# One order and one choice of buffers replaced by another: gated attention and its channel mixer on one TensorE

## The chip, the cores and the metric

The program runs on 1 core of a Trainium2 chip. The metric is device microseconds of one execution. Three runs of the kernel before took 421.2, 421.72 and 422.78 us; the median is 421.72 us. One further execution was taken by the hardware profiler, and every duration below is from it.

## The reference

Four batches, 8 heads, 768 time steps, head width 48, all in float32. Attention is a recurrence over time on a complex state, and its result is the input of a mixer with squared-ReLU and a sigmoid gate:

```
scale = minimum(mag, 0.999) / (mag + 1e-06)          # mag = |a_re + i a_im|
S_re, S_im = ar*S_re - ai*S_im + k (x) v, ar*S_im + ai*S_re
y[t] = q[t] @ S_re                                   # -> x: [batch, time, 8*48]
xk = mu_k*x + (1-mu_k)*x_prev;  xr = mu_r*x + (1-mu_r)*x_prev
v = maximum(xk @ w_k, 0)**2 @ w_v                    # 384 -> 1024 -> 384
out = sigmoid(xr @ w_r) * v
```

## The kernel before, in words

**Units.** The work is cut into eight units u = 0 to 7 of 384 time steps (two for each batch). A unit has three parts. `gate(u)` is work of ScalarE and VectorE: it loads a_re, a_im, k and q (`g`), takes logarithms, scans them over time (L668, L695), and multiplies k and q by the exponentials and by cosine and sine (L685, L730). Its intermediate tiles are called `m`, `ph`, `sq` and `r`. `attend(u)` is TensorE's work on small tiles: transposes of k (`tr`), sums of k times v for the state (`up`), scores (`sc`, masked by VectorE to `pt` at L986) and values (`y`). ScalarE takes the values out of PSUM to `xt` and `ys` (L1046). `mix(u)` makes `xk` and `xr` from `xt` and multiplies them by the weights.

**The mixer on TensorE.** From unit 1 on, each float32 factor is split in two float32r parts (`x` at L361 and L364, `h` at L441 and L445, `w` at L559 and L562), and each product is three matmuls over 128 rows and 384 columns. A product of one 128-row block, `z` (L388), is 9 matmuls. ScalarE applies ReLU (`r`, L429) and squares (`h`, L433), and 9 more matmuls (`o`, L469) add it into three accumulators. Unit 0 does its mixer in plain float32 instead (`z` at L384, `o`): its inputs come from L343 on ScalarE and L347 on VectorE, and the whole weights `wx` are put together from 16-bit pieces by a cast on ScalarE (L535) and a VectorE operation (L540).

**Large and small products.** In what follows `z` and `o` are the large products and `tr`, `up`, `sc` and `y` the small ones. All of a kind are emitted by one line or two, and TensorE alternates between both sorts, because `attend(u)` of a unit runs between the mixer products of the unit before it.

**What sets the order.** Every operation is recorded in a `Plan`, and `ORDER` gives each one a number. `Plan.run` emits them by rising number. The five engine queues then run in that order, and semaphores that the framework adds hold each instruction until its inputs and its buffer are ready.

**Buffers.** A tile is taken from a pool by a tag. Five PSUM banks share the tag `ps`, three `x` buffers, four `r`, two `hx` (which hold the split `h`), two `kt`, two `pt`, four `v` and two `g`. Which of them a new tile gets is the framework's pick; a tile whose buffer still has a reader waits.

A second path, which steps through time in a loop, stands behind a test at the end (L1127); it does not run with these inputs.

Of the kernel before, what the change touches and what calls it, by code (L numbers as in the profile page):

```python
# [22 lines left out]
C = H * D  # L23
# [12 lines left out]
YS = 1  # L36
# [132 lines left out]
}  # L169
PIECE = 2  # L170
GP = 2
HB = 2
R_XK = 1
RB = 4
SIG = 2.5
# [1058 lines left out]
```

## Time and profile before

| | us |
|---|---|
| median of three runs | 421.72 |
| span of the profiled execution (first to last instruction) | 420.5 |
| TensorE (PE) busy | 370.6, 88% |
| VectorE (DVE) busy | 328.6, 78% |
| ScalarE (ACT) busy | 316.6, 75% |
| first matmul starts at | 29.24 |
| last group of matmuls starts at | 409.02 |

The profiled execution has no time of its own beside its span: its 420.5 us stand 1.2 us below the median, and the rest of a run lies around the span.

How to read it. PE, DVE, ACT and SP are TensorE, VectorE, ScalarE and the queue of SyncE that issues the DMAs. PEld is TensorE's loading of weights, which overlaps its matmuls. A busy PE is not a PE at its peak, because matmuls are pipelined and their ends are modelled; from one group's start to the next group's start is the sound measure of how long a group took. [...]

### The profile page before, as it was taken

What the parts mean: (1) busy time and instruction counts of PE and PEld (TensorE: products, weight loads), DVE (VectorE), ACT (ScalarE), POOL (GpSimd) and SP (SyncE); (2) the same over time, 40 slices, a digit from 0 to 9 for tenths busy, and PEclk for the clock granted to TensorE, in tenths of its full rate; (3) what the DMA queues carried; (4) which work ended last, traced back from release to release, by engine and by line L of the source; (5) the groups of instructions that cost most, each with busy time, mean ns of one, the idle gap of its engine ahead of it and who ended that gap; (6) DMA issues with size and microseconds to landing.
All of it is one profiled execution on the core that took longest, in us unless ns stands there. A gap on an engine that the chain in (4) does not pass through costs nothing.

```text
span 420.5 us, 13399 instructions
## 1 busy us (share of the span) xinstructions
PE 370.6 (88%) x5705; PEld 333.5 (79%) x5705; DVE 328.6 (78%) x528; ACT 316.6 (75%) x620; POOL 8.2 (2%) x32
## 2 busy tenths in 40 slices
PE   0018849998999999999999999999999999999992
PEld 0017725776689999999999999899999999999991
DVE  3988899698899989888999789889979694564231
ACT  6999998976998899679987996789776833345221
POOL 6000000000000000000000000000000000000000
PEclk9999969998999999999999999999999999999998
DMA  7998462451444082334343353513140440100101
GB/s 257 412 373 209 133 223 77 89 187 45 142 104 148 8 256 57 86 153 143 82 127 139 133 139 105 228 29 89 49 107 4 105 95 19 53 0 2 57 2 65
DMA packets 22996, 49.72 MB, mean 118 GB/s; under 512 B 4848, under 2 KB 16368, under 8 KB 22928
## 3 DMA queue, kind: packets, MB, share of 16 engines
q1 hardware_dynamic: 22928, 48.78, 37.3%
q8 instruction: 47, 0.77, 0.8%
q14 instruction: 21, 0.17, 0.1%
HBM read 31.06 MB, written 4.72 MB: 85 GB/s over the span
## 4 chain that ended last, share of the span: by engine, by line
PE 63%; ACT 19%; DVE 5%; issue 4%; DVEq 0%; ACTq 0%
PE z L388 25%; PE o L469 17%; PE y L1011 8%; PE up L853 4%; PE sc L970 3%; ACT L248 2%; ACT sq L255 2%; PE tr L821 2%; ACT ph L255 1%; ACT r L255 1%; PE sc L965 1%; ACT r L429 1%; ACT h L433 1%; PE z L384 1%; ACT x L361 1%
## 5 line engine op out<-in xcount | busy, mean ns | idle before, releaser
L388 PE MATMUL z<-x,w 128*128 128x384 f32 x693 | 130.6, 340 | 0.5 <-ACT kt L834 0.4
L388 PEld LDWEIGHTS z<-x,w 128*128 128x128 f32 x693 | 119.4, 188 | 2.7 <-ACT kt L834 0.7
L469 PE MATMUL o<-hx,w 128*128 128x384 f32 x504 | 99.4, 342 | 0.0
L469 PEld LDWEIGHTS o<-hx,w 128*128 128x128 f32 x504 | 86.2, 188 | 1.1
L429 ACT ACTIVATE r<-z 128x384 f32<-128x384 f32 x64 | 30.5, 488 | 32.6 <-PE z L388 28.3
L970 PE MATMUL sc<-g 48*64 48x64 f32 x1200 | 26.1, 228 | 30.9 <-DVE g L730 29.8
L970 PEld LDWEIGHTS sc<-g 48*64 48x64 f32 x1200 | 23.3, 137 | 34.6 <-DVE g L730 30.0
L730 DVE TENSOR_TENSOR g<-g,r 128x768 f32<-128x768 f32 (+1 forms) x24 | 41.5, 1755 | 6.7 <-ACT r L255 6.4
L441 DVE CAST hx<-h 128x384 fp32r<-128x384 f32 x44 | 16.1, 366 | 28.9 <-ACT h L433 17.1
L433 ACT ACTIVATE h<-r 128x384 f32<-128x384 f32 x64 | 33.1, 526 | 2.8 <-DMA out_t<-y 1.6
L255 ACT ACTIVATE sq<-m 128x1152 f32<-128x1152 f32 (+1 forms) x30 | 28.3, 970 | 6.7 <-DVE m L651 4.6
L445 DVE TENSOR_TENSOR hx<-h,hx 128x384 fp32r<-128x384 f32 x56 | 30.4, 553 | 2.2 <-PE z L388 1.5
L248 ACT ACT_TABLE_LOAD x24 | 30.8, 1283 | 1.2 <-PEq L1223 0.8
L361 ACT CAST x<-xm 128x384 fp32r<-128x384 f32 x42 | 21.3, 515 | 11.6 <-DVE xm L353 6.3
L384 PE MATMUL z<-x,wx 128*128 128x384 f32 x66 | 24.4, 524 | 5.4 <-DVE x L347 5.4
L364 DVE TENSOR_TENSOR x<-xm,x 128x384 fp32r<-128x384 f32 x42 | 23.0, 553 | 7.8 <-ACT x L361 7.6
L1011 PE MATMUL y<-q,state 112*48 112x64 f32 (+1 forms) x704 | 25.4, 226 | 3.1 <-ACT xt L1046 1.9
L1011 PEld LDWEIGHTS y<-q,state 112*48 112x48 f32 (+1 forms) x704 | 22.8, 133 | 6.4 <-issue 4.0
L353 DVE SCALAR_TENSOR_TENSOR xm<-dx,mu_sb,xt 128x384 f32<-128x384 f32 x42 | 25.4, 614 | 0.6
L853 PEld LDWEIGHTS up<-v,kt 64*48 64x48 f32 (+1 forms) x1216 | 21.5, 127 | 5.1 <-issue 3.0
L384 PEld LDWEIGHTS z<-x,wx 128*128 128x128 f32 x66 | 13.4, 208 | 14.5 <-issue 7.3
L853 PE MATMUL up<-v,kt 64*64 64x48 f32 (+1 forms) x1216 | 24.0, 217 | 0.0
(89 smaller groups left out, 557.6 us busy)
## 6 DMA issues: line engine op xcount, KB each, us to landing
g<-in_gat SPq DMA_DIRECT2D x18, 768.0 KB, 5.7
raw<-in_w_all SPq DMA_DIRECT2D x9, 767.8 KB, 10.1
g<-in_gat SPq DMA_DIRECT2D x12, 384.0 KB, 8.1
v<-in_vt SPq DMA_DIRECT2D x24, 192.0 KB, 3.5
out_t<-y SPq DMA_DIRECT2D x24, 192.0 KB, 2.5
q<-g SPq DMA_DIRECT2D x84, 48.0 KB, 2.2
q<-g SPq DMA_DIRECT2D x28, 144.0 KB, 3.1
q<-g SPq DMA_DIRECT2D x40, 72.0 KB, 2.3
```

Of the source, the lines that this page charges most:

```text
L248: nc.scalar.add_instruction(mybir.InstLoadActFuncSet(name=nc.get_next_instruction_name(), act_func_set_id=n, engine=mybir.EngineType.Activ ...
L255: nc.scalar.activation(out=out, in_=in_, func=func, **kw)
L384: nc.tensor.matmul(z, lhsT=wx[s[0]][:, s[1]], rhs=hi[which][:, ct], start=ct == 0, stop=ct == NT - 1)
L388: nc.tensor.matmul(z, lhsT=wt[s[0]][:, part, s[1]], rhs=r[which][:, ct], start=n == 0, stop=n == 3 * NT - 1)
L429: nc.scalar.activation(out=t["r", j], in_=t["f", j], func=AF.Relu, scale=1.0 / W_SCALE)
L433: nc.scalar.activation(out=t["h", j], in_=t["r", j], func=AF.Square)
L445: nc.vector.tensor_tensor(out=t["lo", j], in0=t["h", j], in1=t["hi", j].bitcast(F32), op=ALU.subtract)
L469: nc.tensor.matmul(tiles["o", mt], lhsT=w, rhs=r, start=j == 0 and n == 0, stop=j == NJ - 1 and n == len(parts) - 1)
L730: nc.vector.tensor_tensor(out=g[:, d, 2 * i:2 * i + 2], in0=g[:, d, 2:4], in1=t["r"][:, 1 - i, d].unsqueeze(2).to_broadcast([P, k, 2, U]), ...
L853: nc.tensor.matmul(t["up", c, s][i * HR:(KR if i else HR), h * D:(h + 1) * D], lhsT=keys, rhs=V[u][c][r, h * D:(h + 1) * D], start=True, s ...
L970: nc.tensor.matmul(y, lhsT=g[:, 2 * i, q], rhs=g[:, 2 * i + 1, q], start=i == 0, stop=i == 1)
L1011: nc.tensor.matmul(t["y", team][s][rows, h // 2 - team[0], c], lhsT=lhsT[:, cols], rhs=rhs, start=(s, h % 2) not in begun, stop=stop)
```

## The change

All numbers of `ORDER` are replaced by others. The operations, their shapes and their engines are the same. A second table, `HOMES`, states for each tile that takes turns on a few buffers which of them it uses, and each buffer becomes a tag of its own, with one tile at a time. The numbers of buffers stay (five PSUM banks, three `x`, four `r`, two of each of the rest). Of the order's table one row stands here for all.

```
--- before.py
+++ after.py
-    ("w", 0): (36, 41,),
+    ("w", 0): (54, 62,),
...
+BANKS = dict(ps=PB, x=XB, r=RB, hx=HB, kt=KB, pt=PTS, v=VB, g=GB)
+HOMES = {
+    "g": "01010101",
+    "kt": "010101101001001010010101",
...
+    def home(self, slot):
+
+        tag, n = slot
+        return f"{tag}{self.homes[tag][n] if tag in self.homes else n % BANKS[tag]}"
...
-    ps = ctx.enter_context(pool("ps", 5, space=PSUM))
+    ps = ctx.enter_context(pool("ps", 1, space=PSUM))
...
+    def bank(slot, name):
+        return ps.tile([P, 512], F32, tag=home(slot), name=name)
...
-                t["f", j] = ps.tile([P, 512], F32, tag="ps", name="z")[:, :U]
+                t["f", j] = bank(sp, "z")[:, :U]
...
-                t["hx", j] = mp["h"].tile([P, 2, U], F32R, tag="hx", name="hx", bufs=HB)
+                t["hx", j] = mp["h"].tile([P, 2, U], F32R, tag=home(sx), name="hx")
...
+            plan[0].homes = HOMES
             plan[0].run(ORDER)
```

Three places show what the new order does. Line numbers after the change are higher by 29 to 36. In the rows a shape is that of the output, as partitions by elements.

On ScalarE (ACT), ahead of unit 0's mixer. `hx<-raw` is a cast for the weights, `sq` a step of unit 1's gate, `xt` and `ys` the values taken from PSUM, `x<-xt` the inputs of unit 0's first product. Before:

```order
L535 CAST hx<-raw 128x768
L535 CAST hx<-raw 128x384
L1046 ACTIVATE xt,stat<-y 48x3x64 x4
L343 ACTIVATE x<-xt,mu_98 128x384
L255 ACTIVATE sq<-m 128x3x384
L343 ACTIVATE x<-xt,mu_98 128x384 x2
L255 ACTIVATE sq<-m 128x3x384
```

After:

```order
L570 CAST hx<-raw 128x768 x2
L378 ACTIVATE x<-xt,mu_98 128x384 x2
L1081 ACTIVATE xt,stat<-y 48x3x64 x4
L378 ACTIVATE x<-xt,mu_98 128x384 x2
L284 ACTIVATE sq<-m 128x3x384 x2
```

The gate step that stood between the inputs stands behind them. In all, two casts for weights (one of 768 columns, one of 384) and one gate step that stood ahead of the third input of the first product stand behind it, and one more `x<-xt` stands ahead of it.

On ScalarE again, at the values of unit 1. Here `ph` is the arctangent of unit 2's gate, behind a load of its function table. Before:

```order
L255 ACTIVATE sq<-m 128x3x384 x2
L248 ACT_TABLE_LOAD
L255 ACTIVATE ph<-ph 128x1152
L1046 ACTIVATE xt,stat<-y 112x2x3x64 x2
L1046 ACTIVATE ys,stat<-y 112x3x64 x2
```

After:

```order
L1081 ACTIVATE xt,stat<-y 112x2x3x64
L284 ACTIVATE sq<-m 128x3x384 x2
L277 ACT_TABLE_LOAD
L284 ACTIVATE ph<-ph 128x1152
L1081 ACTIVATE xt,stat<-y 112x2x3x64
```

One of the two takings of `y` moved ahead of four gate instructions.

On TensorE, at the second half of unit 4's attention. Before, ahead of the scores and in the middle of the values:

```order
L853 MATMUL up<-v,kt 48x48 x2
L469 MATMUL o<-hx,w 128x384 x9
L388 MATMUL z<-x,w 128x384 x18
L970 MATMUL sc<-g 64x64 x24
L965 MATMUL sc<-q_93 64x64 x12
L1011 MATMUL y<-q_92,state_87 64x64
...
L1011 MATMUL y<-pt,v 48x64 x2
L469 MATMUL o<-hx,w 128x384 x9
L1011 MATMUL y<-q_93,state_87 64x64
```

After:

```order
L888 MATMUL up<-v,kt 48x48 x2
L423 MATMUL z<-x,w 128x384 x54
L504 MATMUL o<-hx,w 128x384 x9
L423 MATMUL z<-x,w 128x384 x27
L504 MATMUL o<-hx,w 128x384 x9
L1046 MATMUL y<-q_92,state_87 64x64
...
L1046 MATMUL y<-pt,v 48x64 x2
L1005 MATMUL sc<-g 64x64 x24
L1000 MATMUL sc<-q_93 64x64 x12
L1046 MATMUL y<-q_93,state_87 64x64
```

Scores and values now follow each other without a large product between them, and the large products stand together in longer runs. Over the whole order, TensorE goes from a small product back to a large one 59 times before (24 of them from a transpose) and 30 times after (14 from a transpose). Runs of 18 or more `o` matmuls: 2 before; 14 after, of which 4 have 27.

## Rows read from the trace of the kernel before

**Rows 1.** Waits of PE: waiter, line, releaser, total us, times, longest.

```profile
PE z L384 <- DVE x L347: 5.4, 1, 5.4
PE y L1011 <- ACT xt L1046: 1.9, 1, 1.9
```

**Rows 2.** Busy us in stretches: PE, PEld, DVE, ACT, POOL, granted clock, DMA share, GB/s.

```profile
42.00:63.00 21.00, 13.76 (x346) 10.46 (x339) 18.71 (x38) 20.16 (x45) 0.38 (x1) 0.84 0.53 176
...
105.00:126.00 21.00, 20.57 (x239) 15.23 (x238) 18.09 (x27) 20.94 (x37) 0.00 (x0) 1.00 0.45 123
...
127.00:409.00 282.00, 281.40 (x4247) 266.91 (x4245) 221.69 (x356) 201.08 (x400) 1.36 (x13) 1.00 0.30 90
```

**Rows 3.** PE in order of time: start, us, group; ahead of unit 0's mixer and in it.

```profile
52.70 0.56 PE L1011 MATMUL y<-pt,v 64*64 64x64 f32 x24
58.66 9.89 PE L384 MATMUL z<-x,wx 128*128 128x384 f32 x24 [5.39 <-DVE x L347]
68.39 2.10 PE L469 MATMUL o<-h,wx 128*128 128x384 f32 x6
```

**Rows 4.** ACT in order of time, ahead of unit 0's mixer.

```profile
52.48 1.55 ACT L535 CAST hx<-raw 128x768 f16<-128x768 bf16 x2
...
56.01 0.62 ACT L343 ACTIVATE x<-xt,mu 128x384 f32<-128x384 f32 x1
56.53 1.15 ACT L255 ACTIVATE sq<-m 128x1152 f32<-128x1152 f32 x1
57.58 1.11 ACT L343 ACTIVATE x<-xt,mu 128x384 f32<-128x384 f32 x2
```

**Rows 5.** PE in order of time, around unit 1's values.

```profile
96.20 2.04 PE L1011 MATMUL y<-q,state 112*64 112x64 f32 x40 [1.87 <-ACT xt L1046]
...
99.66 4.32 PE L384 MATMUL z<-x,wx 128*128 128x384 f32 x12
103.82 2.10 PE L469 MATMUL o<-h,wx 128*128 128x384 f32 x6
105.75 4.03 PE L384 MATMUL z<-x,wx 128*128 128x384 f32 x12
109.62 2.10 PE L469 MATMUL o<-h,wx 128*128 128x384 f32 x6
```

**Rows 6.** ACT in order of time, around unit 1's values.

```profile
93.22 1.28 ACT L248 ACT_TABLE_LOAD   x1
...
95.59 0.48 ACT L1046 ACTIVATE xt<-y 112x384 f32<-112x384 f32 x1
```

**Rows 7.** PE in order of time: large products between large ones, then between small ones.

```profile
192.28 1.72 PE L469 MATMUL o<-hx,w 128*128 128x384 f32 x9
193.84 1.72 PE L388 MATMUL z<-x,w 128*128 128x384 f32 x9
...
229.44 1.84 PE L469 MATMUL o<-hx,w 128*128 128x384 f32 x9
231.21 1.38 PE L1011 MATMUL y<-q,state 112*64 112x64 f32 x40
```

**Rows 8.** PE in order of time: values ahead of scores, scores, values ahead of a large product.

```profile
176.06 1.61 PE L1011 MATMUL y<-q,state 112*64 112x64 f32 x48
...
178.35 1.02 PE L970 MATMUL sc<-g 48*64 48x64 f32 x48
...
183.52 1.61 PE L1011 MATMUL y<-q,state 112*64 112x64 f32 x48
...
185.90 3.42 PE L388 MATMUL z<-x,w 128*128 128x384 f32 x18
```

**Rows 9.** Groups by shape: VectorE making `hx`, and its longest operation. Busy, mean ns, idle before.

```profile
L730 DVE TENSOR_TENSOR g<-g,r 128x2304 f32<-128x2304 f32 x12 | 30.7, 2555 | 5.7 <-ACT r L255 5.4
...
L445 DVE TENSOR_TENSOR hx<-h,hx 128x384 fp32r<-128x384 f32 x56 | 30.4, 553 | 2.2 <-PE z L388 1.5
...
L441 DVE CAST hx<-h 128x384 fp32r<-128x384 f32 x44 | 16.1, 366 | 28.9 <-ACT h L433 17.1 <-PE o L469 10.4 <-ACT m L622 1.3
```

More of the change, by code (lines that the diff above doesn't have):

```diff
@@ L35 @@
 NS = 6
-YS = 1
 NW = NT + 2 * NJ
@@ L49 @@
 ORDER = {
[21 rows of a table removed]
[21 rows of a table added]
     ("f", 0): (4,),
[1 row of a table removed]
[1 row of a table added]
     ("f", 2): (28,),
[95 rows of a table removed]
[97 rows of a table added]
 }
 PIECE = 2
-GP = 2
 HB = 2
+XB = 3
+GB = 2
+VB = 4
+KB = 2
+PB = 5
 R_XK = 1
@@ L183 @@
 FIRST_LOAD = 2
+BANKS = dict(ps=PB, x=XB, r=RB, hx=HB, kt=KB, pt=PTS, v=VB, g=GB)
+HOMES = {
+    "g": "01010101",
+    "hx": "0101010101010101101010101000101010101011010101101010101010",
+    "kt": "010101101001001010010101",
+    "ps": (
+        "300312232340210243411043211402142001234144123233220141432103134030230204302120103104112433400134"
+        "123440120331014022212401241231230103421021103024411430241220440341143204010022120241431430042401"
+        "32134242003433124314213201330042431313102024024104331440311002"
+    ),
+    "pt": "01000110011001101001010101010101",
+    "r": (
+        "100231302130232120132033103201230130230121103010211302201311023033101232012302030132202031323031"
+        "22110312101030211013030332012321033000123231023121003210"
+    ),
+    "v": "103021103302031201301210",
+    "x": "012011122021021011021012201201210200210210200210100201201011011",
+}
 ST_X = 0
@@ L194, in __init__ @@
     def __init__(self):
-        self.ops, self.data, self.slots, self.phase = [], {}, {}, None
+        self.ops, self.data, self.slots, self.phase, self.homes = [], {}, {}, None, {}
     def slot(self, tag):
@@ L260, in op, with home @@
         plan[0].op(f, reads, writes)
+    def home(slot):
+        return plan[0].home(slot)
+    def bank(slot, name):
+        return ps.tile([P, 512], F32, tag=home(slot), name=name)
     def op_act(n, f, psum=False, **kw):
@@ L311, in open_mix @@
         mp["x"] = stack.enter_context(pool("xhl"))
-        mp["h"] = stack.enter_context(pool("hp", 2))
-        mp["t"] = stack.enter_context(pool("xp", 2))
+        mp["h"] = stack.enter_context(pool("hp"))
+        mp["t"] = stack.enter_context(pool("xp"))
     X, x_slot, zr, zr_slot = {}, {}, {}, {}
@@ L331, in delta @@
             def delta():
-                d[ct] = mp["t"].tile([P, U], F32, tag="x", name="dx", bufs=3)
+                d[ct] = mp["t"].tile([P, U], F32, tag=home(sd), name="dx")
                 nc.vector.tensor_tensor(out=d[ct], in0=X[u][:, ct, 1:U + 1], in1=X[u][:, ct, 0:U], op=ALU.subtract)
@@ L349, in whole_new, with one @@
                         in1=hi[which][:, ct], op0=ALU.mult, op1=ALU.add)
-                def one(which=which):
-                    xm[which, ct] = mp["t"].tile([P, U], F32, tag="x", name="xm", bufs=3)
+                def one(which=which, sx=sx):
+                    xm[which, ct] = mp["t"].tile([P, U], F32, tag=home(sx), name="xm")
                     nc.vector.scalar_tensor_tensor(
@@ L401, in mul @@
             def mul():
-                tiles["z", mt] = ps.tile([P, 512], F32, tag="ps", name="z")[:, :U]
+                tiles["z", mt] = bank(sp, "z")[:, :U]
                 product(tiles["z", mt], 1, [(W_R + ct, ts(mt, P)) for ct in range(NT)])
@@ L406, in out_ @@
                 if u not in zr:
-                    zr[u] = mp["h"].tile([P, NT, U], F32, tag="zr", name="zr", bufs=1)
+                    zr[u] = mp["h"].tile([P, NT, U], F32, tag="zr", name="zr")
                 nc.scalar.copy(out=zr[u][:, mt], in_=tiles["z", mt])
@@ L423, in mul @@
             def mul():
-                t["f", j] = ps.tile([P, 512], F32, tag="ps", name="z")[:, :U]
+                t["f", j] = bank(sp, "z")[:, :U]
                 product(t["f", j], 0, [(W_K + 2 * j, ts(ct, P)) for ct in range(NT)])
             def relu():
-                t["r", j] = mp["h"].tile([P, U], F32, tag="r", name="r", bufs=RB)
+                t["r", j] = mp["h"].tile([P, U], F32, tag=home(sr), name="r")
                 nc.scalar.activation(out=t["r", j], in_=t["f", j], func=AF.Relu, scale=1.0 / W_SCALE)
             def square():
-                t["h", j] = mp["h"].tile([P, U], F32, tag="r", name="h", bufs=RB)
+                t["h", j] = mp["h"].tile([P, U], F32, tag=home(sh), name="h")
                 nc.scalar.activation(out=t["h", j], in_=t["r", j], func=AF.Square)
             def h_hi():
-                t["hx", j] = mp["h"].tile([P, 2, U], F32R, tag="hx", name="hx", bufs=HB)
+                t["hx", j] = mp["h"].tile([P, 2, U], F32R, tag=home(sx), name="hx")
                 t["hi", j] = t["hx", j][:, 0]
@@ L484, in mul @@
             def mul():
-                tiles["y", mt] = mp["h"].tile([P, U], F32, tag="r", name="y", bufs=RB)
+                tiles["y", mt] = mp["h"].tile([P, U], F32, tag=home(sr), name="y")
                 nc.vector.scalar_tensor_tensor(out=tiles["y", mt], in0=tiles["o", mt], scalar=1.0 / W_SCALE,
@@ L496, in tile_kernel @@
     with ExitStack() as fast:
-        gp = fast.enter_context(pool("gp", GP))
+        gp = fast.enter_context(pool("gp"))
         tp = fast.enter_context(pool("tp", 1))
-        ap = fast.enter_context(pool("ap", 2))
+        ap = fast.enter_context(pool("ap"))
         xtp = fast.enter_context(pool("xt", 1))
@@ L508, in tile_kernel @@
         hx_slot, upper = [], []
-        for _ in range(HB):
-            x = mp["h"].tile([P, 2, U], F32R, tag="hx", name="hx", bufs=HB)
+        for i in range(HB):
+            hx_slot.append(slot("hx"))
+            x = mp["h"].tile([P, 2, U], F32R, tag=f"hx{i}", name="hx")
             nc.gpsimd.memset(x.bitcast(F32), 0.0)
@@ L529, in convert @@
             n = s.stop - s.start
-            sx = slot("hx") if i < HB else hx_slot[i - HB]
-            hx_slot.append(sx)
+            sx = hx_slot[i % HB]
             def f0():
@@ L580, in f @@
                     if u not in G:
-                        G[u] = gp.tile([P, NT, 4, U], F32, tag="g", name="g")
+                        G[u] = gp.tile([P, NT, 4, U], F32, tag=home(g_slot[u]), name="g")
                     nc.sync.dma_start(out=G[u][:, ct, part], in_=gat[b, half, ct, :, part])
@@ L587, in f @@
                 def f():
-                    v = ap.tile([P, C], F32, tag="v", name="v", bufs=4)
+                    v = ap.tile([P, C], F32, tag=home(v_slot[u][c]), name="v")
                     nc.sync.dma_start(out=v, in_=vt[b, half, c])
@@ L818, in f0 @@
                     def f0():
-                        t["tr", c, part] = ps.tile([P, 512], F32, tag="ps", name="tr")[:rows, :C]
+                        t["tr", c, part] = bank(sp, "tr")[:rows, :C]
                         for ct in range(NT):
@@ L825, in kt @@
                         if ("kt", c) not in t:
-                            t["kt", c] = ap.tile([P, 2 * C + 4 * D], F32, tag="kt", name="kt")
+                            t["kt", c] = ap.tile([P, 2 * C + 4 * D], F32, tag=home(sk), name="kt")
                         return t["kt", c]
@@ L845, in up @@
                     for s in subs:
-                        t["up", c, s] = ps.tile([P, 512], F32, tag="ps", name="up")[:KR, :C]
+                        t["up", c, s] = bank(su[s], "up")[:KR, :C]
                     for h in range(H):
@@ L880, in f0 @@
                     def f0():
-                        t["tr", p, part] = ps.tile([P, 512], F32, tag="ps", name="tr")[:, :C].rearrange(
+                        t["tr", p, part] = bank(sp, "tr")[:, :C].rearrange(
                             "p (c r) -> p c r", c=NC)
@@ L888, in f1 @@
                         if ("kt", p) not in t:
-                            t["kt", p] = ap.tile([P, 2 * C + 4 * D], F32, tag="kt", name="kt")[:, :2 * C].rearrange(
+                            t["kt", p] = ap.tile([P, 2 * C + 4 * D], F32, tag=home(sk), name="kt")[:, :2 * C].rearrange(
                                 "p (i c r) -> p i c r", i=2, c=NC)
@@ L894, in f2 @@
                         if "kt67" not in t:
-                            t["kt67"] = mp["h"].tile([P, NT, U], F32, tag="zr", name="kt67", bufs=1).rearrange(
+                            t["kt67"] = mp["h"].tile([P, NT, U], F32, tag="zr", name="kt67").rearrange(
                                 "p a u -> p (a u)")
@@ L909, in up @@
                     for s in range(2):
-                        t["up", p, s] = ps.tile([P, 512], F32, tag="ps", name="up")[:KR, :NC * 2 * D].rearrange(
+                        t["up", p, s] = bank(su[s], "up")[:KR, :NC * 2 * D].rearrange(
                             "p (c x) -> p c x", c=NC)
@@ L955, in f0 @@
                 def f0():
-                    t["sc", team] = sc = [ps.tile([P, 512], F32, tag="ps", name="sc")[:, :m * U // 2].rearrange(
-                        "p (a c q) -> p a c q", a=m, c=NC) for _ in range(2)]
+                    t["sc", team] = sc = [bank(s, "sc")[:, :m * U // 2].rearrange(
+                        "p (a c q) -> p a c q", a=m, c=NC) for s in sp]
                     for a, p in enumerate(team):
@@ L981, in f1 @@
                         if k not in t:
-                            t[k] = ap.tile([P, 2, NC, SB], F32, tag="pt", name="pt", bufs=PTS)
+                            t[k] = ap.tile([P, 2, NC, SB], F32, tag=home(pt_slot[team[0]][k[2]]), name="pt")
                         o = t[k] if m == 2 else t[k][:, j:j + 1]
@@ L1004, in f0 @@
                 def f0():
-                    t["y", team] = [ps.tile([P, 512], F32, tag="ps", name="y")[:, :m * U // 2].rearrange(
-                        "p (a c q) -> p a c q", a=m, c=NC) for _ in range(2)]
+                    t["y", team] = [bank(s, "y")[:, :m * U // 2].rearrange(
+                        "p (a c q) -> p a c q", a=m, c=NC) for s in sp]
                     begun = set()
@@ L1043, in f @@
                             if "ys" not in t:
-                                t["ys"] = ap.tile([P, 1, NC, 2, SB], F32, tag="ys", name="ys", bufs=YS)
+                                t["ys"] = ap.tile([P, 1, NC, 2, SB], F32, tag="ys", name="ys")
                             o = t["ys"][:KR, :, :, s]
@@ L1125, in tile_kernel @@
         nc.vector.tensor_reduce(out=good, in_=ok, axis=mybir.AxisListType.XY, op=ALU.add)
-        n = ps.tile([P, 512], F32, tag="ps", name="n")[:1, :1]
+        n = ps.tile([P, 512], F32, tag="ps0", name="n")[:1, :1]
         nc.tensor.matmul(n, lhsT=good, rhs=ones1, start=True, stop=True)
```

234 rows, old and new, of the table ORDER are left out of this document.

## The prediction

> **What bounds the kernel now.** I read the waits of PE first. Once it has begun, PE waits little: 5.4 us once for an input of unit 0's mixer and 1.9 us once for a PSUM bank that ScalarE had not emptied [rows 1]. Then the stretches: from 127 to 409 us PE is busy 281.4 of 282 us, while VectorE is busy 221.7 (79%) and ScalarE 201.1 (71%) [rows 2]. Before that the other engines set the pace: ScalarE is busy 20.16 of 21 us in 42 to 63 us and 20.94 of 21 in 105 to 126 us [rows 2]. So the kernel has a head in which ScalarE limits and a long body in which PE does. Last I read PE in order of time, group by group, for what a group costs next to another kind [rows 7, 8]: a full PE can still be filled with fewer microseconds.
>
> **Part 1: the first product of unit 0's mixer.** The last values of unit 0 end at 52.70 + 0.56 = 53.26 us, and the first mixer product starts at 58.66, released by VectorE's last step on the input [rows 1, 3]. VectorE had its operand from ScalarE, which ran, one behind the other, two casts for weights, the takings, one input, a gate step, two inputs [rows 4]. After the change both casts' worth of work and one gate step stand behind these inputs, and one input more ahead. The two casts are 1.55 us busy, some 1.45 from start to start; the gate step is 57.58 - 56.53 = 1.05; an input is 56.53 - 56.01 = 0.52 [rows 4]. ScalarE is full here, so what leaves its queue ahead of the input shows: 1.45 + 1.05 - 0.52 = 2.0 us. Bounds: 0, if VectorE or the values are late in its place, to 3.4, the stretch 5.4 less the two inputs and four takings that must follow the values (some 2 us). I take 2.0, since the rows price just what moves. PE still idles over 3 us here. [...]
>
> The casts moved back must run later, during unit 0's mixer; that is in part 4.
>
> **Part 2: the values of unit 1.** PE has begun them, then waits 1.87 us for ScalarE to empty a bank [rows 1, 5]. ScalarE was loading a function table at 93.22 and took the bank only at 95.59 [rows 6]. After the change one of the two takings stands ahead of two gate steps, the table load and the arctangent, and what precedes it is a weight cast. So the wait goes. With it goes what came behind it: the 88 matmuls left took 99.66 - 96.20 = 3.46 us [rows 5], where 96 of the kind take 185.90 - 183.52 = 2.38 [rows 8], so 88 would take 2.2; and the next 12 took 103.82 - 99.66 = 4.16 against 3.87 [rows 5]. That is 1.9 + 1.3 + 0.3 = 3.5 us. Bounds: 0, if another bank is the late one, to 3.5. I take 3.5, because the instructions that held the taking now follow it. Late next is the second taking, still behind the table load, but the values need one bank besides the free one.
>
> **Part 3: fewer changes between small and large products.** A group of 9 large matmuls takes 193.84 - 192.28 = 1.56 us between large groups and 231.21 - 229.44 = 1.77 between small ones [rows 7]: 0.21 more. The small group pays too: values take 2.38 us ahead of a large product and 178.35 - 176.06 = 2.29 ahead of scores [rows 8], 0.09 more. One excursion from the large products costs 0.30 us beyond its own work. I counted the returns to a large product in PE's order: 59 before, 30 after. Of these 24 and 14 come from transposes, whose three or six matmuls fill the change themselves; I count them at nothing, with 10 x 0.21 = 2.1 us as the other end. That leaves 35 - 16 = 19 excursions at 0.30 us: 5.7 us. Nearly all lie behind 127 us, where nothing but PE is full, so they count whole. Bounds: 0 to 7.8.
>
> The row on PE's busy time would forbid this term: 281.4 of 282 us leaves 0.6 [rows 2]. [...]
>
> **Part 4: what gets late instead.** PE would come to 105 to 126 us 2.0 + 3.5 = 5.5 us earlier, and there ScalarE has 0.06 us to spare in 21 [rows 2]; it also has the casts of part 1 to catch up with. What it fails to deliver early PE waits for. Bounds: 0, as ScalarE has idle time ahead of that stretch, to 5.5, when all of the lead is lost. I take 3.0, a little over half, as the full stretch is the nearest row. Behind 127 us a body shorter by 5.7 us raises VectorE to 80% and ScalarE to 73%; average load hides that, so I add nothing (the third rival is where it does not hold).
>
> Stating the buffers adds no instruction, and their numbers stay; what the choice is worth is in the waits above. On SP, unit 0's third block of k and q now stands behind three more loads of weights. PE begins with the other two blocks, so I cost it at nothing; were that cover gone, it could take back part 1's 2.0 us.
>
> **Sum.** 420.5 - 2.0 - 3.5 - 5.7 + 3.0 = 412.3 us of span. The span is 1.2 us under the median of the runs, so 413.5 us. Its own range, from the bounds of part 4 and some of part 3: 410.5 to 416.5.
>
> **The rivals.**
>
> First, a full PE gains nothing: what a group saves, the next one waits for, as the operands of the large products come at VectorE's and ScalarE's pace. For it speaks the busy row [rows 2]; against it that groups of equal size differ by their neighbours alone [rows 7]. Then 5.7 is lost: 419.2 us.
>
> Second, no new waits at all: the idle share of ScalarE and VectorE takes up everything. For it: 29% and 21% of the body are idle; against it: the full stretch at 105 us [rows 2]. Then 3.0 is not lost: 410.5 us, or 408.4 with the transposes' 2.1.
>
> Third, slower: the longer runs starve. `o` runs of 18 or more matmuls go from 2 to 14, and only two buffers hold their operand `hx`. When a product ends, its buffer is refilled by a VectorE cast and a difference, 0.366 + 0.553 = 0.92 us, under the 1.56 us of the next product. With the longest VectorE operation in front, 2.555 us [rows 9], PE waits 0.92 + 2.56 - 1.56 = 1.9 us. At 12 more such runs that is at most 23 us. It decides from 8.2 / 12 = 0.7 us a run on; at 1.0 us a run the time is 425.5. Against it: VectorE is idle a fifth of the body, and the mean wait is for the rest of an operation, not for a whole one. [...]
>
> Fourth, the table of buffers only writes down what the framework did and the new order shifts waits about: 421.7 us. Against it: the two waits of rows 1 have a cause that the order moves.
>
> **Chances.** Forecast 0.50; first rival 0.14; second 0.20; third 0.10; fourth 0.06. A measurement of this kernel can tell about 0.5% from no change, 2.1 us: 419.6 to 423.8 counts as the same. The forecast, the second rival and most of the first (0.11) are faster: 0.81; the fourth and 0.03 of the first the same, and 0.01 of the third: 0.10; the rest slower: 0.09. The range 408 to 420 holds the first three cases and leaves out the last two.
>
> **What would show it.** Part 1: the first mixer product of unit 0 starts near 56.7 us instead of 58.66. Part 2: the wait of PE for `xt` at unit 1's values is gone, and the granted clock falls once, not twice. Part 3: groups of 9 still take 1.56 and 1.77 us, and the body's PE time shrinks by their number. Part 4: new waits of PE for ScalarE or VectorE between 60 and 127 us, some 3 us in all. The forecast is wrong if PE's waits behind 127 us come to several microseconds, above all inside long `o` runs, or if the first product starts no earlier.

## The result, and the profile after

The kernel after took 415.55 us (median of five runs, 414.87 to 418.63) against 421.72 us before: ratio 0.9861, 95% interval 0.9824 to 0.9897. Run again later it gave 0.9873, 0.9825 to 0.9920. The forecast of 413.5 us with its range of 408 to 420 holds, but not with the sum that it was made of. The profiled execution after has a span of 416.9 us and is the slowest of its five runs, so it shows 3.6 us of the 6.2 by which the medians differ.

PE's waits after, as in [rows 1]:

```profile
PE z L419 <- DVE x L382: 3.9, 2, 2.3
PE sc L1005 <- issue: 3.4, 3, 1.4
PE o L504 <- issue: 1.3, 1, 1.3
PE sc L1000 <- issue: 0.9, 1, 0.9
PE up L958 <- ACT kt L933: 0.9, 1, 0.9
PE z L423 <- issue: 0.7, 1, 0.7
```

The wait for `xt` is gone, the one for the input of unit 0's mixer has become two (3.9 us in all, 5.4 before), and there is a new kind, "issue": the engine waited for nothing that the profile shows. The stretches of [rows 2]:

```profile
42.00:63.00 21.00, 16.75 (x323) 12.97 (x320) 17.85 (x32) 19.00 (x40) 0.75 (x1) 0.88 0.58 201
105.00:126.00 21.00, 20.99 (x310) 16.95 (x309) 20.44 (x30) 20.94 (x37) 0.00 (x0) 1.00 0.39 109
127.00:409.00 282.00, 275.11 (x4176) 265.46 (x4175) 220.48 (x354) 202.08 (x400) 1.75 (x13) 1.00 0.31 89
```

In the first, ScalarE (fourth number) is no longer full, 19.00 instead of 20.16 us. In the second, PE (first number) is full, beside a ScalarE as full as before. In the body PE is busy 6.3 us less (281.40 before), so the new waits stand where the forecast had put none. The granted clock, a share of full speed, stands at 1.00 or 0.50 in the records of both profiles. Ahead of 127 us it falls to 0.50 once, from 57.8 to 64.7 us; before it fell twice, from 55.7 to 62.5 and from 96.7 to 100.1.

PE ahead of unit 0's mixer, and then ScalarE there, as in [rows 3, 4]:

```profile
53.12 0.56 PE L1046 MATMUL y<-pt,v 64*64 64x64 f32 x24
55.32 0.88 PE L419 MATMUL z<-x,wx 128*128 128x384 f32 x2 [1.64 <-DVE x L382]
58.49 10.40 PE L419 MATMUL z<-x,wx 128*128 128x384 f32 x22 [2.28 <-DVE x L382]
```

```profile
51.30 0.33 ACT L1081 ACTIVATE xt<-y 112x192 f32<-112x192 f32 x1 [0.70 <-PE y L1046]
...
52.07 1.99 ACT L570 CAST hx<-raw 128x768 f16<-128x768 bf16 x2
53.92 1.11 ACT L378 ACTIVATE x<-xt,mu 128x384 f32<-128x384 f32 x2
55.05 0.33 ACT L1081 ACTIVATE xt<-y 48x192 f32<-48x192 f32 x1
...
57.17 1.12 ACT L378 ACTIVATE x<-xt,mu 128x384 f32<-128x384 f32 x2
```

The product runs without a break from 58.49 us on, 58.66 before. Two casts and two inputs still stand ahead of the last takings, which begin 1.37 us behind the end of the values. PE at unit 1's values, as in [rows 5]:

```profile
94.04 1.58 PE L1046 MATMUL y<-q,state 112*64 112x64 f32 x48 [0.37 <-DMA q<-g]
95.55 0.91 PE L1046 MATMUL y<-pt,v 64*64 64x64 f32 x48
96.40 3.82 PE L419 MATMUL z<-x,wx 128*128 128x384 f32 x11
...
116.67 5.21 PE L423 MATMUL z<-x,w 128*128 128x384 f32 x27
```

96 values take 96.40 - 94.04 = 2.36 us, at a granted clock of 1.00. The first product of split factors (L423) starts at 116.67, in the kernel before (L388) at 120.38:

```profile
120.38 3.38 PE L388 MATMUL z<-x,w 128*128 128x384 f32 x18
```

The matmuls behind that start are the same 4,297 in both, so it cuts the two executions at the same place of the work. Groups of 9 large matmuls, as in [rows 7]:

```profile
134.83 1.83 PE L504 MATMUL o<-hx,w 128*128 128x384 f32 x9
136.59 1.38 PE L1046 MATMUL y<-q,state 112*64 112x64 f32 x40
...
277.65 1.72 PE L504 MATMUL o<-hx,w 128*128 128x384 f32 x9
279.21 3.28 PE L423 MATMUL z<-x,w 128*128 128x384 f32 x18
```

1.76 us between small groups and 1.56 between large ones: unchanged. Last, one of the new waits:

```profile
241.89 1.14 PE L888 MATMUL up<-v,kt 64*64 64x48 f32 x64
242.86 1.39 PE L1005 MATMUL sc<-g 48*64 48x64 f32 x74
245.61 0.68 PE L1005 MATMUL sc<-g 48*64 48x64 f32 x22 [1.35 <-issue]
246.22 0.84 PE L856 MATMUL tr<-ident,g 128*64 128x128 f32 x6
```

It stands in the middle of one block of scores that had begun 2.75 us earlier. A count of TensorE's records (each product is a weight load and a matmul) tells what such waits have in common. The profile's list of queues has this line (packets, MB, share of 16 engines):

```profile
q8 instruction: 47, 0.77, 0.8%
```

47 packets of 16 KB, for 11,534 instructions of TensorE: about one packet for 256. The waits of the kernel after that are over 0.9 us, with the packets' own records in the trace:

```
first instruction  stopped   packet           starts   packet's end  the 256 before
behind the wait    at us     from, to us      at us    to start      took us
 3777 = 14*256+193  140.06   138.81, 139.71   141.08   1.37          6.15
 4289 = 16*256+193  159.18   157.92, 159.01   160.42   1.41          2.03
 7105 = 27*256+193  244.03   243.11, 244.40   245.61   1.21          2.00
 7873 = 30*256+193  268.47   267.60, 268.50   270.10   1.60          4.57
 8897 = 34*256+193  298.34   296.93, 298.15   299.55   1.40          2.06
10433 = 40*256+193  344.13   342.74, 343.77   345.26   1.49          2.38
```

Theory F: TensorE waits for its own instructions. 256 of them in small products alone were used up in 2.0 us (2.00 to 2.06 at 159, 244 and 298 us). In this trace the next packet mostly began a little behind the first instruction of a new 256 (0.2 to 1.8 us behind it, for 21 of the 34 packets behind 120 us), and at four of these six waits it was 3.3 to 3.6 us from there to the first instruction of the next 256. The theory rests on this trace's packets and TensorE's records alone.

### The profile page after: what moved, and what is told of

Same layout as the page of the kernel before. It is cut to its first block, busy times and chain, and to the rows that moved or that the text cites. A ratio compares the mean times of both kernels' runs of the same rounds, so it can differ in the third digit from the quotient of the medians.

```text
span 416.9 us, 13389 instructions
## 1 busy us (share of the span) xinstructions
PE 370.2 (89%) x5705; PEld 337.3 (81%) x5705; DVE 331.1 (79%) x528; ACT 317.2 (76%) x620; POOL 9.2 (2%) x32
## 4 chain that ended last, share of the span: by engine, by line
PE 65%; ACT 13%; DVE 11%; issue 4%; DMA 3%; SPq 3%; DVEq 0%; ACTq 0%
PE z L423 21%; PE o L504 20%; PE y L1046 6%; PE z L419 5%; PE sc L1005 4%; ACT sq L284 3%; PE up L888 3%; PE tr L856 3%; DVE g L765 2%; SPq L794 2%; ACT L277 2%; DVE ph L730 1%; ACT ph L284 1%; DMA xt<-ys 1%; DMA q<-g 1%
## 5 line engine op out<-in xcount | busy, mean ns | idle before, releaser
L423 PE MATMUL z<-x,w 128*128 128x384 f32 x693 | 127.5, 338 | 0.7 <-issue 0.7
L423 PEld LDWEIGHTS z<-x,w 128*128 128x128 f32 x693 | 119.6, 188 | 2.6 <-ACT xt L1081 0.9
L504 PE MATMUL o<-hx,w 128*128 128x384 f32 x504 | 95.2, 339 | 1.3 <-issue 1.3
L504 PEld LDWEIGHTS o<-hx,w 128*128 128x128 f32 x504 | 87.1, 188 | 2.0 <-issue 1.6
L919 PE MATMUL tr<-ident,g 128*128 128x128 f32 x18 | 5.0, 433 | 27.9 <-DVE stat L739 27.3
L419 PE MATMUL z<-x,wx 128*128 128x384 f32 x66 | 25.4, 542 | 3.9 <-DVE x L382 3.9
L1005 PEld LDWEIGHTS sc<-g 48*64 48x64 f32 x1200 | 24.5, 143 | 5.1 <-issue 4.8
L919 PEld LDWEIGHTS tr<-ident,g 128*128 128x128 f32 x18 | 3.2, 216 | 28.8 <-issue 27.7
L1046 PEld LDWEIGHTS y<-q,state 112*48 112x48 f32 (+1 forms) x704 | 23.7, 137 | 3.4 <-issue 1.9
L388 DVE SCALAR_TENSOR_TENSOR xm<-dx,mu_sb,xt 128x384 f32<-128x384 f32 x42 | 25.5, 615 | 0.7
```

Of the source, the lines that this page charges most:

```text
L388: nc.vector.scalar_tensor_tensor(out=xm[which, ct], in0=d[ct], scalar=mu_sb[:, which, ct:ct + 1], in1=X[u][:, ct, 0:U], op0=ALU.mult, op1= ...
L419: nc.tensor.matmul(z, lhsT=wx[s[0]][:, s[1]], rhs=hi[which][:, ct], start=ct == 0, stop=ct == NT - 1)
L423: nc.tensor.matmul(z, lhsT=wt[s[0]][:, part, s[1]], rhs=r[which][:, ct], start=n == 0, stop=n == 3 * NT - 1)
L504: nc.tensor.matmul(tiles["o", mt], lhsT=w, rhs=r, start=j == 0 and n == 0, stop=j == NJ - 1 and n == len(parts) - 1)
L1005: nc.tensor.matmul(y, lhsT=g[:, 2 * i, q], rhs=g[:, 2 * i + 1, q], start=i == 0, stop=i == 1)
L1046: nc.tensor.matmul(t["y", team][s][rows, h // 2 - team[0], c], lhsT=lhsT[:, cols], rhs=rhs, start=(s, h % 2) not in begun, stop=stop)
```

## The experiments

**Where the waits stand.** Three kernels with matmuls of one element ahead of TensorE's first product (98 and 128 in the kernel after, 83 in the kernel before):

```
+            d = pso.tile([P, 512], F32, tag="o0", name="d")[:1, :1]
+            for _ in range(98):
+                nc.tensor.matmul(d, lhsT=ones1, rhs=ones1, start=True, stop=True)
```

> The kernel after the change, with 98 matmuls of one element ahead of TensorE's first product (it is idle there until 27 us); nothing else changes. Theory F: each unexplained wait of the kernel after stands where the count of TensorE's instructions passes 256 n + 193, and ends 1.2 to 1.6 us behind a 16 KB transfer of instructions; TensorE waits for its next 256 instructions when it used up the last 256, all of small products, in some 2 us. 98 matmuls are 196 instructions, so the places move by 196 (to 256 n - 3 of the old count) and fewer runs of small products hold two of them: worked out from the trace of the kernel after, 3.4 us of waits instead of 7.2, so 3.8 us faster than the kernel after, and the waits at 159, 244, 298 and 344 us are at other matmuls. Rival B (the scores wait for a PSUM bank or a buffer whose reader is late): the waits stay at the same matmuls with the same lengths, time as the kernel after within 0.5 us.

> As the run before, with 128 matmuls of one element ahead: 256 instructions, so the places where a new 256 begins stay at the same matmuls. Theory F: the same waits at the same matmuls as in the kernel after, time as the kernel after within 1 us. It is the control for the added matmuls themselves: were it as much faster as the run with 98, the gain would be theirs (a warmer TensorE, say). Rival B: also no change.

> The kernel before the change, with 83 matmuls of one element ahead of TensorE's first product. Theory F: in the kernel before nearly no stretch of 256 instructions holds small products alone, with the places where they are; moved by 166 instructions, about three do, and the waits worked out from its trace rise from near 0 to 3.7 us: 2 to 4 us slower than the kernel before. Rival B: no change, within 0.5 us.

Each of these matmuls leaves four records, not the two that had been counted on: the traces hold 392 more with 98, 512 with 128 and 332 with 83. So the places moved by 136 with 98 and by 76 with 83, not by 196 and 166; with 128 they stayed, and there are two more packets, 49.

With 128: 415.07 us, ratio 0.9823 (0.9787 to 0.9860), and every wait is at the matmul where it was; the one at 268 us is absent. With 98: 416.04, 0.9846 (0.9802 to 0.9891), and every one has moved to 256 n + 193 of the new count. PE with 98, at the scores that had stopped at 159.18 us, and at others that now stop:

```profile
156.75 1.14 PE L888 MATMUL up<-v,kt 64*64 64x48 f32 x64
157.72 1.74 PE L1005 MATMUL sc<-g 48*64 48x64 f32 x96
159.38 0.55 PE L856 MATMUL tr<-ident,g 128*128 128x128 f32 x3
...
337.40 1.68 PE L1005 MATMUL sc<-g 48*64 48x64 f32 x94
340.44 1.66 PE L1005 MATMUL sc<-g 48*64 48x64 f32 x50 [1.36 <-issue]
```

Rival B is out: the same scores with the same banks run through. The size was missed: the body's waits are 5.0 us with 98 and 5.7 with 128, not 3.4 and 7.2, and the times can't be told apart. The kernel before with 83 did not slow down (423.22 us, 1.0011, 0.9985 to 1.0037): no 256 instructions behind 70 us took it less than 3.2 us, and its waits at 256 n + 193 behind its first split product come to 0.25 us.

The sizes expected belong to places that were not tried. An estimate for the places that were: each 256 in the trace that takes less than 3.3 us waits for the rest of these 3.3. It gives 4.5 us for the kernel after with 98 (5.0 measured) and 0.1 for the kernel before with 83 (0.25 measured); moved by 166, that kernel would have had 3.8. So the order before has such stretches too, and they cost it little because of where its count stands. Over 64 places, 4 records apart, the estimate runs from 0 to 3.8 us (mean 1.1) for the order before and from 3.3 to 8.2 (mean 5.5) for the order after. Beyond the places above no run tests it.

**The order without the table of buffers.** The kernel before with the numbers of the new order alone.

> The new order with the framework's pick of buffers, without the table of buffers. If the order makes the whole difference (theory): as the kernel after within 1 us, the same waits at the same instruction counts. If the stated buffers carry part of it (rival): slower than the kernel after by waits of TensorE for banks or of VectorE and ScalarE for x, r and hx, with releasers named in the profile, 1 to 6 us, which would put it between the two kernels or behind the kernel before.

418.59 us, 0.9910 (0.9877 to 0.9942): between the two. The intervals meet, so the table is worth between nothing and some 4 us. Its profile has the waits for instructions at the same places, without the one at 268 us, 6.8 us in the body, and behind the one of 1.83 us at 244 us this:

```profile
247.33 6.49 PE L471 MATMUL o<-hx,w 128*128 128x384 f32 x27
253.66 8.66 PE L390 MATMUL z<-x,w 128*128 128x384 f32 x49
```

```profile
247.00:250.00 3.00, 3.00 (x15) 3.00 (x13) 2.29 (x5) 0.51 (x2) 0.00 (x0) 0.59 0.52 120
```

The granted clock fell, to 0.59 on average in these 3 us; 27 matmuls took 253.66 - 247.33 = 6.33 us, in the run with 128 ahead 4.77. Here the wait cost 1.6 us more than itself. All three waits for instructions of over 1.8 us that these profiles hold behind 127 us were followed by a fall of the clock, two of ten between 1.4 and 1.65 us, and none of the shorter ones.

**Part 2 undone, and part 2 alone.** In the kernel after, the arctangent's and the taking's numbers (the taking behind the gate steps again); in the kernel before, the taking's:

```
 after   ("g", 2) arctangent 389 -> 385.5   ("a", 1) taking 378 -> 385.9
 before  ("a", 1) taking 389 -> 379.5
```

> The kernel after, with one thing undone on ScalarE at unit 1's values: the first taking stands again behind two gate steps, the table load and the arctangent, as in the kernel before. Theory (part 2 of the forecast): TensorE waits for a bank again at the second half of unit 1's values, some 3 us now because it comes there earlier, and the granted clock falls a second time: 3 to 5 us slower than the kernel after, near 419. Rival (ScalarE in 105 to 126 us takes the lead back in either case): the wait comes back, but the time is within 1 us of the kernel after.

> The kernel before with one instruction moved on ScalarE and nothing else: at unit 1's values the first taking stands ahead of the two gate steps, the table load and the arctangent. Theory (part 2 carries most of the change): TensorE's wait of 1.87 us for the bank goes, the clock does not fall behind it, and the time falls by 3.5 us, up to the 5 us by which the kernel after grew when this move was undone: 417 to 418. Rival (the full ScalarE at 105 to 126 us takes the lead back, the change's gain is in the merged runs): within 1 us of the kernel before. Rival (another bank is late): the wait stays in part, 1 to 2 us faster.

Undone: 420.69 us, 0.9971 (0.9938 to 1.0005), by the ratios some 4.5 us above the kernel after. The wait is back, and the clock falls a second time, at 95 us (and a third at 249, behind a wait for instructions of 1.84 us):

```profile
91.96 0.43 PE L1041 MATMUL y<-q,state 112*64 112x64 f32 x8 [0.90 <-DMA q<-g]
95.22 2.39 PE L1041 MATMUL y<-q,state 112*64 112x64 f32 x40 [2.83 <-ACT xt L1076]
```

Alone: 419.98 us, 0.9968 (0.9938 to 0.9998), a gain of 1.4 us and not the 3.5 to 5 expected. Around the values it gains 3.57 us, as the rows said: from 90.91 to 103.82 us before (12.91) and from 92.14 to 101.48 now (9.34). But at 118 us 1.2 of it is gone again; the stretch of the full ScalarE:

```profile
105.00:126.00 21.00, 19.83 (x239) 14.97 (x238) 19.97 (x29) 20.94 (x37) 0.00 (x0) 1.00 0.46 126
```

PE is busy 19.83 us there, 20.57 in [rows 2]. So part 4's loss is real in the old order; in the new one PE is busy 20.99 us there.

**Part 1 tried again.** ScalarE's two casts behind the inputs of unit 0's first product. The first trial moved one input behind them as well, whose VectorE step stands ahead of the others.

```
 first   casts 218, 223 -> 245.3, 245.6   input ct1 243 -> 233.5   input for the gate 231 -> 245.8
 second  casts 218, 223 -> 245.3, 245.6   input for the gate 231 -> 245.2, its VectorE step 246 -> 249.2
 both    VectorE's step for the first cast 236 -> 249.4
```

> The kernel after, with the two weight casts of ScalarE (1.85 us from start to start) and one input for the gate product moved behind the inputs of unit 0's first mixer product, the second of these inputs ahead of the takings, and VectorE's weight step for the first cast likewise behind. Theory (part 1 of the forecast failed because the casts still stand ahead of the last takings): the product starts in earnest near 57.0 us instead of 58.49, so 1.5 us faster than the kernel after, if the weights are not late in their turn. Rival (the start is set by the values' end and VectorE, not by the casts): still 58.5 us and no change; or the casts now delay a later step of the gate or the weights and PE gives it back by 127 us: within 0.5 us of the kernel after.

> The casts again, without the mistake of the first trial, in which VectorE's queue stood for 4.9 us at a step whose input had been moved behind the casts. Now, from the kernel after: the two weight casts of ScalarE behind the three inputs of the first product of unit 0's mixer and behind the one input for the gate product, VectorE's steps for both likewise behind its three. Theory: the takings start at 53.5 us instead of 55.05, the product starts in earnest at 57.1 instead of 58.49, 1.4 us faster than the kernel after. Rival (later steps give it back, the casts being late for the gate product's weights or the first split product): the start is earlier, the time within 0.5 us of the kernel after.

The first: 419.99 us, 0.9948 (0.9915 to 0.9981), a product that starts at 61.44, since VectorE's queue stood 4.88 us at that step. The second: 414.95 us, 0.9831 (0.9798 to 0.9864). PE, and ScalarE:

```profile
57.22 10.37 PE L414 MATMUL z<-x,wx 128*128 128x384 f32 x22 [1.67 <-DVE x L377]
```

```profile
53.78 0.33 ACT L1076 ACTIVATE xt<-y 48x192 f32<-48x192 f32 x1 [1.67 <-PE y L1041]
...
55.90 1.63 ACT L373 ACTIVATE x<-xt,mu 128x384 f32<-128x384 f32 x3
57.44 1.95 ACT L565 CAST hx<-raw 128x768 f16<-128x768 bf16 x2
```

1.27 us earlier than in the first profile of the kernel after, where the values end at the same 53.7 us, and still 1.36 at 131 us. Later the clock fell in this execution, at 244 us. But other profiles with the order after start this product anywhere from 56.9 to 58.8 us (the table below), and by the times alone the gain is not shown.

**The three longest waits split.** One large group between `up` and `sc` of units 3, 5 and 6:

```
 ("m", 1) o j=6  653 -> 665.5    ("m", 3) o j=4  1015 -> 1033.5    ("a", 6) sc (0, 1)  1261 -> 1270.5
```

> The kernel after, with one group of 9 large matmuls between the state sums (up) and the scores (sc) at the three places where TensorE waited 1.2 to 1.6 us in the middle of the scores (units 3, 5 and 6, at 159, 244 and 298 us). Theory F (the next 256 instructions are not there yet, since the last 256 were all of small products): the three waits of 1.24, 1.57 and 1.21 us go, each split costs 0.30 us for the excursion: 4.0 - 0.9 = 3.1 us faster than the kernel after, and the clock no longer falls behind them; the waits at the other instruction counts stay. Rival B (a late bank or buffer): the waits move with the scores or stay; time within 0.5 us, or 0.9 us slower by the excursions. Rival E (an excursion costs nothing, the merging never paid): 4.0 us faster.

> The edits of the three splits and of the casts together. Theory: the gains add, 3.1 + 1.5 = 4.6 us faster than the kernel after, near 411. Rival (what is won ahead of 60 us is lost at the full ScalarE by 127 us): as the three splits alone.

> The mended casts and the three splits together: the version that the runs so far point to. The casts start the mixer 1.3 us earlier; the splits take the three longest waits for instructions out and put waits for inputs in their place (no gain by themselves), but no stall of 1.4 us and more is left after which the clock fell to half for 3.4 us in four other runs, at some 1.7 us each. If both add: 1.3 us under the kernel after in the same call, up to 2.5 us if that kernel loses to the clock in most of its executions. Rival (what is won in the head is lost in the body to waits for inputs, which are then longer by the lead): the same as the kernel after within 0.5 us.

> The kernel after the change, unchanged, on the same chip as the run before, as its measure: 415.0 to 415.6 us, with waits where the count of TensorE's instructions passes 256 n + 193, of other lengths than in its first profile but at the same matmuls.

The splits: 415.55 us, 0.9872 (0.9825 to 0.9918). The three waits are gone, and no gain came of it. PE at unit 5:

```profile
235.33 1.81 PE L499 MATMUL o<-hx,w 128*128 128x384 f32 x9
238.56 1.14 PE L883 MATMUL up<-v,kt 64*64 64x48 f32 x64 [1.42 <-ACT kt L860]
239.63 1.84 PE L499 MATMUL o<-hx,w 128*128 128x384 f32 x9
241.40 1.89 PE L1000 MATMUL sc<-g 48*64 48x64 f32 x96
```

`up` now comes a group earlier and waits 1.42 us for ScalarE; at the other two places 1.01, and 0.43 and 0.65: 3.5 us in all, with three excursions more. At the first two the group that moved behind `up` had covered this wait, so the trial put one wait in the place of another and does not price the waits for instructions. With the first casts: 418.70 us, 0.9930 (0.9900 to 0.9959), with a product that starts at 60.46 for the same reason as above. With the mended ones: 415.80 us, 0.9838 (0.9799 to 0.9878), beside 417.25 us, 0.9873, for the kernel after, run beside it (415.0 to 415.6 had been expected): 1.45 us, as the first theory has it, but the intervals overlap. Its runs lie within 414.4 to 416.5 us, those of the kernel after within 412.8 to 418.6.

## Why the forecast held, point by point

The profiles cut the executions in two, at the start of the first split product. Ahead of it:

```
                          unit 0's   its first  the next   first split  from next to
                          values end product    product    product      split, us
before                     53.27     58.66      68.39      120.38       51.99
before, 83 ahead           54.83     60.22      69.56      120.47       50.91
before, taking ahead       54.27     59.66      70.16      119.24       49.08
after                      53.69     58.49      68.73      116.67       47.94
after, again               52.72     56.88      66.71      114.84       48.13
after, 128 ahead           53.68     58.48      68.72      116.40       47.68
after, 98 ahead            54.66     58.80      68.61      116.92       48.31
order alone                54.27     58.70      68.11      116.31       48.20
three splits               54.08     57.82      66.47      114.37       47.90
taking back                52.21     57.13      66.14      118.98       52.84
casts mended               53.70     57.22      67.43      115.27       47.84
```

(The first product's start is that of its unbroken part.) Behind it, with the waits of over 0.2 us at 256 n + 193, and 1.6 us for each fall of the clock, an estimate from the run with the order alone:

```
                           starts   rest of   waits for     half    rest without
                           at us    the span  instructions  clock   both
before                     120.38   300.13    0.56          -       299.6
before, 83 ahead           120.47   298.82    0.25          -       298.6
before, taking ahead       119.24   298.53    0.00          -       298.5
after                      116.67   300.27    8.53          -       291.7
after, again               114.84   296.21    5.27          -       290.9
after, 128 ahead           116.40   297.10    5.69          -       291.4
after, 98 ahead            116.92   298.15    5.01          1.6     291.5
after, casts mended        115.27   299.72    6.61          1.6     291.5
```

The three further profiles of this order without splits give 292.7 (order alone), 291.1 (first casts) and 291.8 (taking back).

**Part 1 (2.0 us) is open in size, and its reason failed.** In the first pair of profiles the product starts 0.17 us earlier, by the forecast's own test almost a failure. But the start varies by up to 2 us among profiles of one order: 58.7 to 60.2 us in three with the head of the order before, 56.9 to 58.8 in seven with that of the order after, on average 1.5 us earlier. From the end of the values it is 5.39 us in all three and 3.7 to 4.9 in the seven. The forecast said "ScalarE is full here, so what leaves its queue ahead of the input shows", and counted both casts among what leaves. But two casts are still there, now both of 768 columns and 1.85 us from start to start, and ScalarE idled 0.70 us for PE at 51.30. What left the queue, between the first taking of this half (51.30, before 50.00) and the product, is two gate steps and two other takings. Nor did the earlier start last in the first pair: the granted clock in this product is 0.70 on average (58.49 to 68.73 us) where it was 0.80 (58.66 to 68.39), and the next product begins at 68.73 instead of 68.39.

**Part 2 (3.5 us) held.** From unit 0's second product to the first split product the order after takes 47.7 to 48.3 us, the order before 50.9 and 52.0: 3.4 us less on average. With the taking put back it is 52.84 again; with the taking ahead alone, 49.08.

**Part 3 (5.7 us) held as a price and failed in "they count whole".** Without the waits for instructions the rest of the span fell by some 7.5 us, from about 298.9 to 291.4. Of this 6.5 lie up to the end of the last large product and 1.0 behind it, where the end of the kernel took 6.3 to 6.4 us instead of 6.8 to 8.1. The groups' prices are unchanged (1.56 and 1.76 us), so by the count the excursions are 5.7 of the 6.5; what the other 0.8 us are was not taken apart. That transposes fill the change themselves was the author's estimate: in the trace of before, 9 large matmuls between two groups of transposes took 1.65 us at eight places of ten, 0.09 more than between large ones. But 5.0 to 8.5 us went to TensorE's own instructions, at times 1.6 more to the clock. Small groups put together save the excursions and make stretches that use up 256 instructions in 2.0 us, where behind 70 us the order before took 3.59 us at the least. That these waits cost their full length is so by this count alone: no run took them out without putting others in their place. By [rows 2] PE had 0.6 us left in the body, by the weight loads 15.1; 6.5 us more fitted. That the term would fit in spite of the 0.6 us was the author's estimate.

**Part 4 (3.0 us lost) failed, in place and in cause.** In 105 to 126 us PE lost nothing (busy 20.99 of 21 us). The loss came behind 127 us, where the forecast said "I add nothing", was larger, and was for TensorE's own instructions, not for ScalarE or VectorE.

So the sum held by luck. Ahead of the split product it has 2.0 + 3.5 - 3.0 = 2.5 us, and 3.7 came in the first pair of profiles, 5.5 in the second profile of the kernel after. Behind it the sum has 5.7; -0.1 came in the first pair, 3.9 in the second. The two errors have opposite signs, and the 6.2 us between the medians lie between the pair's 3.6 and the 9.5 of the second profile.

The first rival's outcome (419.2 us, what a group saves is waited for) is near the profiled execution, with instructions in the place of operands. The third, starving `o` runs, did not occur: their one wait, at 268 us, is one for instructions. By the forecast's own test, waits of several microseconds behind 127 us, its account was wrong there and its time right.

## What to carry to other kernels

Count instructions as well as time. Where TensorE used up 256 instructions of small products in 2.0 us here, it then stood still for 1.2 to 1.6 us; in the order before, with its large products in between and 83 matmuls ahead, no 256 behind 70 us took less than 3.2 us, and such waits came to 0.25 us behind the first split product. There a large product in between was cover as much as it was cost. Where the count stood mattered too: with 98 matmuls of one element ahead, the same order had its waits at other matmuls, 5.0 us of them in the body. A wait whose releaser the profile calls "issue", in the middle of a block, is told from a late bank by its place in the count, and by a few idle instructions ahead that move it; count in the trace how many records these add (four for each here). And compare more than one profile of each kernel before a microsecond is given to a cause: a single taking behind a table load, put back, cost some 4.5 of the 6.2 us that all 1,630 new numbers gained, but moved alone it gained 1.4.

## What had not been expected of the hardware

Packets of 16 KB took 0.9 to 1.6 us each, and at the waits the next instruction started 1.2 to 1.6 us after the packet's end. At two of them, 140 and 268 us, the packet began 4.5 and 3.6 us behind the first instruction of the 256 before it, 0.6 to 1.1 at the other four, without a cause that the profile shows; that stays open. It is also part of why executions of one kernel spread: the two profiles of the kernel after have spans of 416.9 and 411.1 us, and of the 5.9 us between them 3.3 are these waits and 1.8 lie ahead of the first split product.
